# Seven pair products in two more expert half layers of an attention, expert and feed-forward kernel

## Chip, core and metric

The kernel runs on one core of a Trainium2 chip. The metric is the device time of one execution in microseconds (us); the median of three runs of the kernel before is 1067.14 us (1067.11 to 1068.03). All arithmetic is float32; a matrix product is made of three float32r products (high times high, high times low, low times high), so every operand is split into a high part (a float32r copy) and a low part (the rest).

## The reference

```python
x = attention(q, k, v, s)                  # 1152 tokens, 512 wide
P = gate(x @ w_gate)                       # exp, then 8 alternating normalisations, 1152 x 8
for e in range(8):                         # w1[e]: 512 x 1024, w2[e]: 1024 x 512
    out += P[:, e:e+1] * (np.maximum(x @ w1[e], 0) @ w2[e])
h = out @ w_in                             # 512 x 2048, given in float64
return softplus(h) @ w_out                 # 2048 x 512, given in float64
```

## The kernel before

After the attention the work is a row of 20 **half layers**, each with 512 hidden units: 0 to 15 are the experts' (two an expert), 16 to 19 the last layer's. `NX` is 16, `NH` is 20, `XE` is 2. A half layer has two parts.

**Up.** The tokens come in two groups g of 576. For each group the 512 by 512 product is made by a scheme with seven products instead of eight; the names a1 to b7 in the order strings stand for these products (two sets, a and b), each of six matmuls that move 288 columns (L450). That gives 28 products in a half layer. Vector and Scalar combine them and write the hidden values as high and low parts (`hh`, `hl`).

**Down.** In half layers 0 to 15 `downs` multiplies by w2 tile by tile: nine tiles of 128 tokens, four row blocks of w2 each, three matmuls of 512 columns for each (L526), 108 matmuls in all. One such triple is a "d" in the order strings, 36 in a half layer. After a tile's last triple Vector adds it, times the gate, to `acc` (L544). The two banks y1 and y2 alternate between tiles, so a tile can't begin before the add of the tile two before has read its bank.

In half layers 16 to 19 (`SEVEN`, `seven(x)`) the down product of the eight whole tiles also has seven products (`pairs`, L368): for each group 7 products, two row halves each, six matmuls of 256 columns, which is 14 "d" of six matmuls a group and 168 matmuls in all; only the tile that straddles the groups still goes through `downs` (12 matmuls of 512 columns). For this the hidden values are first written as whole words (`hw`, L406), then `h_steps` makes their sums (L303) and high and low parts (L296, L299), and the four sums of w2's blocks lie in `sp_t["th"]` and `sp_t["tl"]`.

**Weights.** For half layers 1 to 15 the raw weights are loaded by SP (`load`, L142) and split while the half layer before runs: `sums1` and `sums2` on GpSimd (L162 to L171) make the block sums of w1, `split` makes high parts on Scalar (L153) and low parts on Vector (L156), `prep2` does the same for w2 (L219, L221; half of the low parts on GpSimd). w2's parts have one buffer, so each row block is replaced as soon as the last tile has used it. For half layers 16 to 19 `convert` makes everything ahead: 16 jobs, each of two `narrow` (64-bit numbers made into float32 by seven Vector operations, one Scalar and one GpSimd operation), four block sums on GpSimd (L1130), and four high parts (Scalar, L1138) and low parts (Vector, L1140), stored to DRAM (`wd`, L1144). `ready1`, `prep_b` and `prep_t` later load them from there with DMAs on SP.

**Order.** The order is written by hand: `play` goes through a string; after every product and every d it calls `step`, which advances the generators of the side work by one yield: `back` (weights), `side` and `bot` (hidden values), the gate's steps in half layers up to 1, and `convert` in half layers 2 to 13 at every second step. Part A of half layer x runs products of (x, group 1) among the d of tiles 0 to 3 (30 steps), part B runs products of (x+1, group 0) among the d of tiles 4 to 8 (34 steps). Every engine works in program order, so an instruction that waits holds what is behind it.

```python
A_SEQ = "a1 b1 a2 b2 =0 d d a6 d d b6 d d a7 d d b7 =1 d a5 d b5 d a3 d b3 d a4 d b4 d d"
B_SEQ = "d d =2 a1 d d b1 d a2 d b2 d a6 d b6 d a7 d b7 d a5 d b5 d d w0 a3 d d w2 b3 d d w1 a4 d d w3 b4"
A7_SEQ = "E0 a1 ~ b1 ~ {22} a2 ~ b2 ~ {21} =0 a6 d b6 d a7 d b7 d F0 =1 a5 d b5 d a3 d b3 d a4 d b4 d"
```

`=0` to `=2` queue the splits of the next half layer's w1, `w0` to `w3` those of its w2, `E` and `F` queue `h_steps`. Where the half layer before was not a seven-product one, `~` and the braces in `A7_SEQ` are empty. At x = 14 what is left of `convert` is run and its memory closed; at the end of half layer 15 `open_blocks` takes memory for `hw`, `th` and the like.

## Time and profile before

| | us |
|---|---|
| median of three runs | 1067.14 |
| the profiled execution | 1068.36 |
| its span, first to last instruction | 1066.6 |
| TensorE busy (matmul) | 1051.5 |
| VectorE busy | 776.1 |
| ScalarE busy | 518.4 |
| GpSimd busy | 341.6 |

The profiled execution is 1.76 us longer than its span and 1.22 us above the median. Matmul records overlap, since a matmul's record lasts longer than the distance to the next; TensorE's pace is therefore read from the chain of work that ended last, where a piece's time is the distance to the next piece. TensorE's granted clock is 0.998 of full speed (2.4 GHz) on average.

### The profile page before, as it was taken

How to read it: one execution, taken by the hardware profiler on the slowest of the kernel's cores; microseconds unless marked ns; L12 is line 12 of the kernel's file. 1: busy time of each engine (PE TensorE's matmuls, PEld its weight loads, DVE VectorE, ACT ScalarE, POOL GpSimd, SP SyncE). 2: the span in 40 equal slices, each digit the busy share in tenths (PEclk: the TensorE clock that was granted, in tenths of full speed). 3: DMA queues.
4: the chain of work that ended last, by engine and by line, in shares of the span. 5: the costliest groups of instructions: out<-in, count | busy, mean ns of one | idle time of the engine just before them, and what ended most of it. 6: DMA issues, size and time to landing. Idle time of an engine off the chain costs nothing.

```text
span 1066.6 us, 18737 instructions
## 1 busy us (share of the span) xinstructions
PE 1051.5 (99%) x6876; PEld 940.2 (88%) x6876; DVE 776.1 (73%) x1713; ACT 518.4 (49%) x1232; POOL 341.6 (32%) x397
## 2 busy tenths in 40 slices
PE   6999999999999999999999999999999999999998
PEld 4777888898898888888898888888898889999998
DVE  5576565777879787898878888788555467577766
ACT  6999544344444444444444435444343247543432
POOL 8885303053543335261543434163220011000000
PEclk9999999999999999999999999999999999999999
DMA  6231101124333534334343433442220244464542
GB/s 199 75 88 57 41 29 52 41 99 128 137 126 125 178 113 164 123 115 139 148 160 101 174 121 137 129 149 75 93 80 1 63 163 151 139 209 153 172 139 89
DMA packets 75827, 124.63 MB, mean 117 GB/s; under 512 B 9184, under 2 KB 45024, under 8 KB 75736
## 3 DMA queue, kind: packets, MB, share of 16 engines
q1 hardware_dynamic: 75552, 123.23, 34.5%
q8 instruction: 54, 0.88, 0.3%
q14 instruction: 37, 0.30, 0.1%
q10 hardware_dynamic: 184, 0.20, 0.1%
HBM read 89.06 MB, written 33.82 MB: 115 GB/s over the span
## 4 chain that ended last, share of the span: by engine, by line
PE 90%; DVE 4%; POOL 2%; issue 2%; ACT 2%; DMA 1%; SPq 0%; POOLq 0%; ACTq 0%; DVEq 0%
PE ph L450 39%; PE py L526 37%; PE py L368 7%; PE sc L742 1%; PE pv L849 1%; POOL eb L805 1%; PE tr L823 1%; PE sc L746 0%; DVE w2l L221 0%; ACT eb L792 0%; DVE acc L544 0%; PE tr L817 0%; PE pv L859 0%; PE pg L1030 0%; DVE c L1105 0%
## 5 line engine op out<-in xcount | busy, mean ns | idle before, releaser
L450 PE MATMUL ph<-xh,w1h 128*128 128x288 f32 x1120 | 331.9, 296 | 0.9 <-DVE t L489 0.5
L450 PE MATMUL ph<-xh,w1l 128*128 128x288 f32 x1120 | 330.8, 295 | 0.0
L450 PE MATMUL ph<-xl,w1h 128*128 128x288 f32 x1120 | 329.3, 294 | 0.0
L526 PE MATMUL py<-w2h,hh 128*128 128x512 f32 x588 | 233.7, 397 | 0.7 <-DVE acc L544 0.7
L526 PE MATMUL py<-w2h,hl 128*128 128x512 f32 x588 | 232.5, 395 | 0.0
L526 PE MATMUL py<-w2l,hh 128*128 128x512 f32 x588 | 232.3, 395 | 0.0
L450 PEld LDWEIGHTS ph<-xh,w1h 128*128 128x128 f32 x1120 | 210.1, 188 | 19.6 <-ACT v L458 1.5
L450 PEld LDWEIGHTS ph<-xl,w1h 128*128 128x128 f32 x1120 | 210.4, 188 | 16.7
L450 PEld LDWEIGHTS ph<-xh,w1l 128*128 128x128 f32 x1120 | 210.2, 188 | 0.0
L417 ACT ACTIVATE hh<-ph 128x288 fp32r<-128x288 f32 x192 | 78.5, 410 | 165.0 <-DVE ph L500 96.1
L458 ACT ACTIVATE v<-ph 128x288 f32<-128x288 f32 x160 | 64.5, 409 | 178.2 <-PE ph L450 175.8
L526 PEld LDWEIGHTS py<-w2h,hl 128*128 128x128 f32 x588 | 110.5, 188 | 26.9 <-DVE hl L424 0.3
L544 DVE SCALAR_TENSOR_TENSOR acc<-py,gate,acc 128x512 f32<-128x512 f32 x126 | 93.7, 744 | 47.1 <-PE py L526 47.1
L526 PEld LDWEIGHTS py<-w2h,hh 128*128 128x128 f32 x588 | 110.4, 188 | 11.3 <-DVE acc L544 1.1
L526 PEld LDWEIGHTS py<-w2l,hh 128*128 128x128 f32 x588 | 110.6, 188 | 9.4
L221 POOL TENSOR_TENSOR w2l<-raw,w2h 128x512 fp32r<-128x512 f32 x32 | 44.6, 1393 | 215.2 <-ACT w2h L219 213.2
L1114 POOL TENSOR_TENSOR c<-c,ct 128x512 f32<-128x512 f32 x32 | 43.3, 1354 | 216.9 <-DVE ct L1111 198.3
L424 DVE SCALAR_TENSOR_TENSOR hl<-ph,hh 128x288 fp32r<-128x288 f32 x192 | 86.5, 452 | 28.4 <-ACT hh L417 26.7
L156 DVE TENSOR_TENSOR w1l<-raw,w1h 128x512 fp32r<-128x512 f32 (+1 forms) x128 | 89.5, 699 | 7.5 <-ACT w1h L153 7.3
L489 DVE TENSOR_TENSOR t<-ph,v 128x288 f32<-128x288 f32 x80 | 36.4, 454 | 63.6 <-ACT v L458 62.9
L153 ACT ACTIVATE w1h<-raw 128x512 fp32r<-128x512 f32 (+1 forms) x128 | 73.1, 571 | 1.6 <-POOL raw L169 1.6
L331 DVE TENSOR_TENSOR acc<-py,acc 128x256 f32<-128x256 f32 x96 | 40.6, 423 | 31.5 <-PE py L368 27.8
(237 smaller groups left out, 1704.2 us busy)
## 6 DMA issues: line engine op xcount, KB each, us to landing
raw<-in_w SPq DMA_DIRECT2D x64, 512.0 KB
wd<-ch SPq DMA_DIRECT2D x56, 256.0 KB
wd<-cl SPq DMA_DIRECT2D x56, 256.0 KB
f<-in_w_in SPq DMA_DIRECT2D x16, 512.0 KB
f<-in_w_out SPq DMA_DIRECT2D x16, 512.0 KB
w1h<-wd SPq DMA_DIRECT2D x24, 256.0 KB
w1l<-wd SPq DMA_DIRECT2D x24, 256.0 KB
th<-wd SPq DMA_DIRECT2D x16, 256.0 KB
```

Source lines behind the costliest of these rows:

```text
L153: nc.scalar.activation(out=hi[:, o], in_=t[:, src], func=AF.Copy)
L156: nc.vector.tensor_tensor(out=lo[:, o], in0=t[:, src], in1=f(hi[:, o]), op=ALU.subtract)
L221: (nc.gpsimd if i else nc.vector).tensor_tensor(out=lo, in0=t[:, r], in1=f(hi), op=ALU.subtract)
L331: nc.vector.tensor_tensor(out=a, in0=py, in1=a, op=ALU.add)
L368: nc.tensor.matmul(o, u, v, start=(start and c == 0 and n == 0), stop=(c == 1 and n == 2), skip_group_check=True)
L417: nc.scalar.activation(out=hh, in_=z, func=AF.Relu)
L424: nc.vector.scalar_tensor_tensor(out=hl, in0=z, scalar=0.0, in1=f(hh), op0=ALU.max, op1=ALU.subtract)
L450: nc.tensor.matmul(o, u, v, start=(start and c == 0 and n == 0), stop=(c == 1 and n == 2), skip_group_check=True)
L458: nc.scalar.activation(out=t, in_=self.a, func=AF.Copy)
L526: nc.tensor.matmul(py[t], u, v, start=(k == 0 and n == 0), stop=(k == NF - 1 and n == 2))
L544: nc.vector.scalar_tensor_tensor(out=a, in0=py, scalar=gate_t[0][:, t, e:e + 1], in1=a, op0=ALU.mult, op1=ALU.add)
L1114: nc.gpsimd.tensor_tensor(out=m, in0=m, in1=f(t), op=ALU.add)
```

## The change

Half layers 13 and 14 join `SEVEN`. What is stored in `wd` is now one tensor a half layer.

- **Weights of 13** are made by a new generator `prepare`, advanced at four of seven steps during half layers up to 1 (beside the gate). For each of four jobs (w1 twice, w2 twice): loads on SP, four block sums on GpSimd, four high parts on Scalar; each low part is a Scalar copy of the negated high part, onto which a DMA issued by GpSimd adds the raw weights (`accum_op`). They are stored by SP with the pool `c0`.
- **Weights of 14** are made by the same generator inside `convert`, ahead of the conversion, with the low parts on Vector.
- **`convert`** is advanced at three of four steps instead of one of two, in half layers 2 to 12, and has to be done at the end of part A of 12 (there `open_blocks` follows) instead of part A of 13. `narrow` gets two more yields, so that no two of its Vector operations come in one step, and stores are issued one block later.
- **Half layer 15** stays as it was, but follows a seven-product one: four of its w1 low parts and its four w2 low parts are made by a negated copy on Scalar and an adding DMA issued by GpSimd.
- The writing of hidden values is put off by counts that `later` gives; the loads of `th`/`tl` for 13 (`y3 y2 y4 y1`) stand in part B of 12.

```diff
-    SEVEN = (NX, NX + 1, NX + 2, NX + 3)
+    SEVEN = (NX - 3, NX - 2, *range(NX, NH))
     def load(x, which, i):
+        while seven(x):
+            x += 1
 # split
-            nc.vector.tensor_tensor(out=lo[:, o], in0=t[:, src], in1=f(hi[:, o]), op=ALU.subtract)
+            if seven(x - 1) and g < 2:
+                nc.scalar.activation(out=lo[:, o], in_=f(hi[:, o]), func=AF.Copy, scale=-1.0)
+                nc.gpsimd.dma_start(out=f(lo[:, o]), in_=t[:, src], accum_op=ALU.add)
+            else:
+                nc.vector.tensor_tensor(out=lo[:, o], in0=t[:, src], in1=f(hi[:, o]), op=ALU.subtract)
 # prep2
-        (nc.gpsimd if i else nc.vector).tensor_tensor(out=lo, in0=t[:, r], in1=f(hi), op=ALU.subtract)
+        if seven(x - 1):
+            nc.scalar.activation(out=lo, in_=f(hi), func=AF.Copy, scale=-1.0)
+            nc.gpsimd.dma_start(out=f(lo), in_=t[:, r], accum_op=ALU.add)
+        else:
+            (nc.gpsimd if i else nc.vector).tensor_tensor(out=lo, in0=t[:, r], in1=f(hi), op=ALU.subtract)
+    def later(x, g, k):
+        if seven(x):
+            return 0 if (x, g) == (NX, 0) else k
+        return 10 if k == 8 and g == 0 and seven(x - 1) else 0
+        def seven_blocks(pool, t, which, x, n, bufs, added):
...
+            for c in range(4):
...
+                nc.scalar.activation(out=h, in_=t[:, u], func=AF.Copy)
+                yield
+                if c in added:
+                    nc.scalar.activation(out=l, in_=f(h), func=AF.Copy, scale=-1.0)
+                    nc.gpsimd.dma_start(out=f(l), in_=t[:, u], accum_op=ALU.add)
+                else:
+                    nc.vector.tensor_tensor(out=l, in0=t[:, u], in1=f(h), op=ALU.subtract)
+                for _ in store:
+                    pass
+                store = put(u, h, l)
+                yield
+        def prepare(pool, xs, bufs):
+            for x in xs:
+                for which, n in ((1, 0), (1, 1), (2, 0), (2, 1)):
...
+                    for _ in range(3):
+                        yield
+                    yield from seven_blocks(pool, t, which, x, n, bufs, range(4) if bufs == 4 else ())
+                    for _ in range(2):
+                        yield
 # convert
-            for _ in range(4):
-                yield
+            yield from prepare(cv, [x for x in SEVEN[1:] if x < NX], 3)
 # step
+                if tick[0] % 7 in (1, 3, 5, 6):
+                    next(first, None)
-            elif x < NX - 2 and tick[0] % 2:
+            elif x < SEVEN[0] and tick[0] % 4:
                 next(conv, None)
 # the half layers
-            if x == NX - 2:
-                for _ in conv:
-                    pass
-                cv.close()
+            if x + 1 == SEVEN[0]:
+                for _ in conv:
+                    pass
+                cv.close()
+                own = open_blocks()
-                play(B_SEQ, products(x + 1, 0), d)
+                play(B_SEQ.replace("b2", "b2 y3 y2 y4 y1") if seven(x + 1) else B_SEQ, products(x + 1, 0), d)
```

## Rows read from the trace of the kernel before

**Rows 1.** The page: span, then busy time, share and instructions of each engine.
```profile
span 1066.6 us, 18737 instructions
...
PE 1051.5 (99%) x6876; PEld 940.2 (88%) x6876; DVE 776.1 (73%) x1713; ACT 518.4 (49%) x1232; POOL 341.6 (32%) x397
```

**Rows 2.** The page: the chain of work that ended last, by engine.
```profile
PE 90%; DVE 4%; POOL 2%; issue 2%; ACT 2%; DMA 1%; SPq 0%; POOLq 0%; ACTq 0%; DVEq 0%
```

**Rows 3.** Busy time by half layer, from one product a1 to the next half's.
```profile
core 0: us, PE busy (x) PEld busy (x) DVE busy (x) ACT busy (x) POOL busy (x), PEclk, DMA share, GB/s
...
148.13:196.40 48.27, 48.27 (x284) 43.16 (x282) 32.20 (x109) 19.68 (x45) 8.43 (x10) 1.00 0.13 44
...
339.35:387.91 48.56, 48.00 (x277) 42.52 (x276) 41.41 (x73) 21.70 (x50) 20.93 (x21) 1.00 0.40 136
...
435.39:483.32 47.93, 47.72 (x277) 42.59 (x276) 41.75 (x74) 21.42 (x50) 22.61 (x21) 1.00 0.39 135
483.32:530.80 47.48, 47.48 (x277) 42.55 (x276) 39.70 (x76) 22.10 (x50) 15.57 (x17) 1.00 0.41 142
...
578.28:626.11 47.83, 47.74 (x277) 42.48 (x276) 40.22 (x74) 23.06 (x51) 16.45 (x16) 1.00 0.46 155
...
721.07:768.55 47.48, 47.48 (x277) 42.56 (x276) 35.22 (x64) 19.63 (x45) 15.18 (x16) 1.00 0.27 89
768.55:816.03 47.48, 47.48 (x277) 42.55 (x276) 24.27 (x47) 18.74 (x41) 8.44 (x10) 1.00 0.13 45
...
911.32:956.13 44.81, 44.81 (x350) 44.27 (x349) 27.84 (x55) 21.92 (x54) 0.00 (x0) 1.00 0.54 177
```

**Rows 4.** Pieces of the chain that ended last: start us, us, what.
```profile
506.43 3.99 PE ph L450 x30
528.17 2.80 PE py L526 x12
...
922.67 1.40 PE py L368 x12
```

**Rows 5.** Who TensorE waited for from 196 to 890 us: total, times, longest.
```profile
PE py L526 <- DVE acc L544: 0.7, 2, 0.5
```

**Rows 6.** Twelve us from the start of part A: half layers 7 and 14.
```profile
459.13:471.13 12.00, 12.00 (x74) 10.81 (x72) 11.81 (x20) 5.06 (x13) 7.42 (x7) 1.00 0.38 133
...
792.29:804.29 12.00, 12.00 (x75) 10.91 (x74) 5.68 (x13) 5.01 (x11) 5.66 (x7) 1.00 0.26 89
```

**Rows 7.** Groups by line and shape: busy us, mean ns, idle before.
```profile
L1130 POOL TENSOR_TENSOR c<-c 128x256 f32<-128x256 f32 x64 | 52.7, 842 | 1.7
...
L500 DVE TENSOR_TENSOR ph<-ph,u 128x288 f32<-128x288 f32 x80 | 36.7, 459 | 19.0 <-PE ph L450 18.6
...
L1138 ACT ACTIVATE ch<-c 128x512 fp32r<-128x512 f32 x56 | 34.6, 625 | 0.9 <-POOL c L1130 0.8
...
L299 DVE TENSOR_TENSOR hl<-hw,hh 128x512 fp32r<-128x512 f32 x32 | 21.9, 685 | 1.7 <-ACT hh L296 1.5
...
L296 ACT ACTIVATE hh<-hw 128x512 fp32r<-128x512 f32 x32 | 20.0, 624 | 3.0 <-DVE hw L303 2.9
L406 ACT ACTIVATE hw<-ph 128x288 f32<-128x288 f32 x48 | 19.0, 409 | 26.3 <-DVE ph L500 14.1 <-PE ph L450 11.4 <-DVE ph L471 0.5
```

**Rows 8.** The chain at the start: the two longest pieces that are DMAs.
```profile
0.74 3.02 DMA xr<-in_s
13.26 2.71 DMA qk<-in_q
```

**Rows 9.** Issues by SP of one kind: duration ns least/median/most, first and last start.
```profile
L1144 SPq DMA_DIRECT2D wd<-ch x64: 319/378/1168, 250.6 to 750.8; - x64
```

**Rows 10.** The first Vector operation of `narrow`, in the same columns.
```profile
L1098 DVE TENSOR_SCALAR f<-f x32: 413/421/1523, 225.1 to 728.5; 128x512 f32<-128x512 f32 x32
```

More of the change, by code (lines that the diff above doesn't have):

```diff
@@ L318, in h_steps @@
                 elif n[0] == "h":
-                    assert n != "hs3" or g or not seven(last[0]) or (*last, "s4 done") in ready
+                    assert n != "hs3" or g and "s3h" in sp_t or not seven(last[0]) or (*last, "s4 done") in ready
                     high(n[1:])
@@ L1068, in gate_steps, with put @@
                 yield
+        def seven_blocks(pool, t, which, x, n, bufs, added):
+            for o, a, b, op in (((4, 0, 3, ALU.add), (6, 1, 0, ALU.subtract), (7, 4, 1, ALU.subtract),
+                                 (5, 2, 7, ALU.subtract)) if which == 1 else
+                                ((4, 1, 0, ALU.subtract), (6, 3, 1, ALU.subtract), (5, 3, 4, ALU.subtract),
+                                 (7, 2, 5, ALU.subtract))):
+                nc.gpsimd.tensor_tensor(out=t[:, o], in0=t[:, a], in1=t[:, b], op=op)
+                if o == 6:
+                    yield
+            yield
+            store = iter(())
+            def put(u, h, l):
+                for k, y in enumerate((h, l)):
+                    d = wd[1, x][n][:, k, u] if which == 1 else wd[2, x][:, k, u, n]
+                    nc.sync.dma_start(out=d, in_=f(y))
+                    yield
+            for c in range(4):
+                o = int(which == 1 and c == 0)
+                u = slice(2 * c + o, 2 * c + 2)
+                h, l = (pool.tile([P, 2, HW], F32R, tag="c" + k, name="c" + k, bufs=bufs)[:, o:] for k in "hl")
+                nc.scalar.activation(out=h, in_=t[:, u], func=AF.Copy)
[8 more added lines that the diff above has]
+                store = put(u, h, l)
+                yield
+            yield
+            for _ in store:
+                pass
@@ new lines, in prepare @@
+        def prepare(pool, xs, bufs):
+            for x in xs:
+                for which, n in ((1, 0), (1, 1), (2, 0), (2, 1)):
+                    t = pool.tile([P, 8, HW], F32, tag="c8", name="c8", bufs=1)
+                    src = ([(t[:, :4], w1[x, n])] if which == 1 else
+                           [(t[:, 2 * i:2 * i + 2], w2[x, i][:, n * DM:(n + 1) * DM]) for i in range(2)])
+                    for o, z in src:
+                        nc.sync.dma_start(out=o, in_=z.rearrange("p (b n) -> p b n", n=HW))
+                    for _ in range(3):
+                        yield
+                    yield from seven_blocks(pool, t, which, x, n, bufs, range(4) if bufs == 4 else ())
+                    for _ in range(2):
+                        yield
@@ L1217, in attention_moe_ffn @@
         conv = iter(())
+        c0 = ExitStack()
+        first = prepare(c0.enter_context(tc.tile_pool(name="c0", bufs=4, reuse_waits="tile")), SEVEN[:1], 4)
         back = []
@@ L1373, in attention_moe_ffn @@
             if x == XE - 1:
-                for _ in gates:
+                for _ in then(gates, first):
                     pass
+                c0.close()
                 gt.close()
```

56 lines of the change are left out of this document (21 added, 35 removed).

## The prediction

> **What bounds the kernel now.** First the busy times: TensorE is busy for 1051.5 of 1066.6 us, Vector is next with 776.1 [rows 1]. Since matmul records overlap, that alone proves nothing, so second the chain of work that ended last: 90% of it is TensorE [rows 2]. Third the length of each half layer. Half layers 8, 13 and 14 take 47.48 us each, to the hundredth, although Vector is busy for 39.70, 35.22 and 24.27 us of them [rows 3]: a length that doesn't move with the load of the others is TensorE's own. The pieces of the chain say the same: 2.80 us for 12 matmuls of 512 columns is 0.233 us each, 3.99 us for 30 of 288 is 0.133 [rows 4], and 168 x 0.133 + 108 x 0.233 = 47.5 us. The half layers that are longer, 5, 7 and 10, have together 1.08 + 0.45 + 0.35 = 1.88 us over 47.48 [rows 3]; they are where Vector is busiest, and what TensorE visibly waited for from 196 to 890 us is Vector's add to `acc`, twice, 0.7 us in all [rows 5]. So: TensorE bounds everything after the attention, and Vector is the engine that could take its place while `convert` runs.
>
> **What the change takes away.** A half layer with seven pair products has 168 matmuls of 256 columns where the other has 96 of 512; the other 12 and the 168 of the up product stay. 12 of 256 columns take 1.40 us, 0.117 each [rows 4]: 96 x 0.233 - 168 x 0.117 = 22.4 - 19.6 = 2.8 us. The stage itself gives a little less: half layer 17, which already has them, takes 44.81 us (18 the same), against 47.48 [rows 3], so 2.67 us. I take the stage, because it holds what the pair products cost in stalls. Two half layers: **-5.34 us**, all of it on the path.
>
> The Trainium skill (TensorE: Matmul & The Clock Gate, Back-to-back issue gap) gives a matmul its columns at 2.4 GHz plus about 2.5 ns. That makes 215.8 and 109.2 ns, and a gain of 96 x 215.8 - 168 x 109.2 = 2.4 us, an estimate from that page, or 4.7 for two; the rows have 233 and 117 ns at the full clock, so here the cost over the columns is not a fixed one, and the rows decide.
>
> **What it adds beside the path.** The steps are the clock of the side work: 64 steps in 47.48 us, 0.742 us each.
>
> (1) `convert`. Before, a job takes 22 yields at every second step: 32 yields a half layer, 1.45 jobs. After, narrow has 8 yields instead of 6 and a job 27; three of four steps are 48 yields a half layer, 1.78 jobs. Need: 4 x 16 for the weights of 14 and 16 x 27 = 496; there are 10 half layers and the 30 steps of part A of 12, 670 x 3/4 = 502. It just fits, so no burst is left for the moment when `convert` is emptied. Vector's price of one job: half layer 8 has 39.70 us of Vector work, 14 without conversion has 24.27 [rows 3], so 15.4 / 1.45 = 10.6 us. After: 24.3 + 1.78 x 10.6 = 43.2 of 47.48 us, 91%, where it was 84%; the busiest half layer so far, 7, has 41.75 us and lost 0.45 [rows 3]. So Vector still has room on average, and what counts are the stretches in which narrow runs. The tightest is early in part A: the first tile's add must free its bank within one d and one product, some 1.5 us after its last matmul, of which the add takes half. Twelve us from the start of part A, Vector has 5.68 us of work without conversion and 11.81 with narrow in it [rows 6]. Narrow's seven Vector operations come in 12 steps before and in 10.7 after, so 6.1 us become 6.9, and 11.8 become 12.6 in 12.0: 0.6 us of backlog more. Against that no step has two of them any more, which takes away up to one operation of lag. Narrow covers 16 of 27 yields, so it meets this place in about 6 of 10 half layers. Bounds: all present stalls gone, -1.9 us; every one of 10 half layers as bad as the worst now, 10 x 1.08 - 1.9 = +8.9. I take **+1.0**, near the low end, as a conversion load of 11.8 in 12 us costs a few tenths today. The weights of 14 add 16 Vector low parts in the first 64 yields; they come where narrow doesn't run yet.
>
> (2) The gate's stretch. 16 high parts and 16 negated copies on Scalar, 32 x 0.625 = 20 us; 16 block sums on GpSimd, 16 x 0.842 = 13.5 us [rows 7]; 16 adding DMAs. Scalar is busy for 19.7 us and GpSimd for 8.4 us of the 48.27 us of half layer 1 [rows 3], so both have room, and 64 of some 80 yields are needed. Such a half layer is 0.8 us over 47.48 now. I take +0.2 (0 to 1.5).
>
> (3) The adding DMA, 24 in all: no row shows a DMA that GpSimd issues. From below, an issue by SP takes 0.32 us [rows 9], and a DMA's whole way at the start of the program takes 2.71 and 3.02 us [rows 8]; from above I put 10 us to landing and one block sum's time or two on GpSimd. I take about 3 us, by rows 8, and no cost: in 14 the copies for 15 are queued 6 to 8 us ahead of the product that needs them, and w2's row block 2, the tightest, some 7 us. What is queued behind: `sums2` on GpSimd overwrites what the DMA reads, so it now waits for the landing; behind it wait the next high parts on Scalar, and behind those Scalar's copies of products. The cover is gone at about 8 us.
> The Trainium skill (DMA: Bandwidth & Descriptors, Anatomy of one DMA) gives this path 2.0 us plus the bytes at 436 GB/s: an estimate of 2.6 us for 256 KB, by which the sum stays. No run here shows it.
>
> (4) The entry into 13. Its first pair product comes five products after the last one of part B of 12, 5 x 0.8 = 4.0 us. Till then: Vector's add 0.46, the word on Scalar 0.41, high part 0.62, low part 0.685 [rows 7], in order with two of Scalar's copies, one more high part and one add, each about 0.4: some 3.6 us. It fits with little room; +0.2 (0 to 1.5). The weights of 13 come by DMA as those of 17 do now; the last block that is needed early, w1's load in the string (row block 1), is issued 3 us before the last product ends and used 4 us after that. Words, sums and parts of 13 and 14 are those of 17, whose stretch leaves Vector 17 us idle [rows 3]; the gate's factor in the 28 adds costs Vector nothing that shows. Vector loses the splits for 13 and 14, which is worth nothing.
>
> **The sum**, against the profiled execution of 1068.36 us: -5.34 + 1.0 + 0.2 + 0.2 = -3.9, so 1064.4; the median of the runs stands 1.22 us below it: **1063.2 us**. What is late next is still TensorE.
>
> **The rivals.**
> No new stall at all: 1067.14 - 5.34 = 1061.8, and with the present ones gone 1059.9. For it: no two Vector operations of narrow in one step. Chance 0.14.
>
> Vector takes the gain back: a backlog in 6 to 10 half layers at the worst loss of today, 1.08 us, and part A's first bank as the place; 6 x 1.08 - 1.9 = +4.6 gives 1066.4, 10 x 1.08 gives 1070.7 at the very most. What speaks for it is 91% on average, over 100% within narrow. One thing could make it so: the first operation of narrow takes 421 ns mostly, and 1523 at most [rows 10]; the 1.1 us between are about one GpSimd operation, and GpSimd's work per half layer grows by the same 22% as the jobs. The Trainium skill (SBUF — State Buffer, Who interferes with whom) has it that such Vector instructions and GpSimd's share a port that one of them holds to the end of its instruction; the trace agrees with its 1523. Chance 0.18, and the time lies mostly within 0.2% of no change.
>
> Slower: the adding DMA takes over about 8.7 us to land. In the gate's stretch one job's tile is loaded anew only after the last such DMA has read it; from that DMA's yield to the next job's first high part there are 9 yields of 1.3 us, 11.7, less 3 for the load. Above that Scalar stands with the high part at its head, and TensorE behind its copies; four jobs in a row, and half layer 15's weights twice. At 12 us: 4 x 3.3 + 2 x 4 = 21, less 5.3: 1083. It decides from about 11 us on (4 x 2.3 + 2 x 3 = 15). Rows 8 speak against it. Chance 0.08.
>
> **How the numbers follow.** Forecast 0.58, no new stall 0.14, Vector 0.18, DMA 0.08, others that are slower 0.02. What a measurement can tell here is 0.2%, 2.1 us: faster is under 1065.0, which the forecast mostly and the second case meet: 0.70; within 0.2%: Vector's case and the upper end of the forecast, 0.19; slower 0.11. Range: from 1060.9, between the two values without new stalls, to 1068.0, which takes in most of Vector's case and leaves the DMA's out.
>
> **What would show it.** Right: half layers 13 and 14 at about 44.8 us each, those from 2 to 12 at 47.5 to 48.1 with TensorE's waits on `acc` of one or two us in all, and no longer gate stretch. Wrong: half layers of 48.5 us and more with Vector full in their part A (Vector's case); gaps of TensorE behind Scalar in half layers 0, 1 and 14, with GpSimd waiting for DMAs (the DMA's case); a gap of over 1 us at the first pair product of 13 would undo (4).

## The result and the profile after

The changed kernel takes **1078.1 us** (four runs, 1077.5 to 1080.0), the one before 1067.1: 1.0104 times as long, interval 1.0092 to 1.0117. The forecast was 1063.2 us, its range 1060.9 to 1068.0. The profiled execution is the longest of the four (1080.0 us), so its parts add up to some 2 us more than the median.

The page of the changed kernel: span, busy time of each engine, and the chain that ended last.

```profile
span 1078.2 us, 19516 instructions
...
PE 1051.5 (98%) x7020; PEld 943.5 (88%) x7020; DVE 818.1 (76%) x1759; ACT 546.7 (51%) x1296; POOL 371.5 (34%) x431
...
PE 69%; DVE 14%; POOL 5%; DMA 4%; issue 4%; ACT 4%; SPq 0%; POOLq 0%; DVEq 0%; ACTq 0%
```

Against [rows 1, 2] TensorE's busy time hasn't moved, although its matmuls became shorter by some 5 us: records around a stall are longer, and count as busy (half layer 8 has 48.78 us for the products that took 47.48 before). Its share of the chain fell from 90 to 69%. That tells which engines the chain runs through, not how long TensorE stood; the table below has that. Busy time by half layer, in the columns of [rows 3]; these are half layers 1, 2, 4, 8, 13 and 14:

```profile
147.58:199.51 51.93, 50.05 (x283) 44.43 (x282) 36.37 (x109) 29.10 (x65) 23.39 (x29) 0.97 0.75 204
199.51:250.62 51.11, 48.12 (x278) 42.62 (x277) 32.30 (x68) 19.03 (x45) 20.37 (x23) 1.00 0.42 142
298.59:347.19 48.60, 47.75 (x277) 42.61 (x276) 44.27 (x79) 22.90 (x52) 22.87 (x22) 1.00 0.45 152
492.75:543.59 50.84, 48.78 (x278) 42.13 (x276) 44.28 (x78) 22.75 (x52) 21.78 (x22) 1.00 0.47 161
737.47:779.41 41.94, 41.94 (x283) 39.48 (x282) 20.13 (x38) 14.47 (x35) 0.00 (x0) 1.00 0.54 180
779.41:824.23 44.82, 44.82 (x351) 44.27 (x350) 32.89 (x65) 23.45 (x53) 5.51 (x7) 1.00 0.45 136
```

Cut finer, from the first product of each part to the first of the next, the two profiled executions differ like this (1A is part A of half layer 1; a row of half layer x above is part B of x - 1 and part A of x). Every part that isn't named differs by less than 0.1 us.

| stretch | after less before, us | forecast |
|---|---|---|
| attention, up to half layer 0 | -1.3 | 0 |
| parts A of half layers 0, 1, 2 | +0.7, +3.7, +3.1 = +7.4 | +0.2 |
| parts A of 3 to 11 | +0.5, +1.1, -1.1, +1.3, +1.4, +3.2, +1.3, +1.0, +1.3 = +10.0 | +1.0 |
| parts B of 2 to 12 | +0.2 | 0 |
| part A of 12 | 0.0 | 0 |
| 13A, 13B, 14A, 14B, 15A | -5.5, +0.1, -2.7, +3.5, 0.0 = -4.7 | -5.3 + 0.2 = -5.1 |
| sum | 11.6 | -3.9 |

The attention's 1.3 us have nothing to do with the change. In the profiled execution before, the granted clock is 0.50 (1.2 instead of 2.4 GHz) from 18.1 to 21.4 us, in that of the changed kernel it is 1.00:

```profile
18.10:21.40 3.30, 3.23 (x18) 2.24 (x16) 0.91 (x6) 2.94 (x10) 3.30 (x5) 0.50 0.91 351
18.10:21.40 3.30, 3.08 (x29) 2.17 (x28) 1.63 (x10) 3.29 (x11) 3.30 (x5) 1.00 0.98 361
```

Nine of the nineteen traces of this document have the low stretch there, and their attention is as long as before to 0.3 us; in the ten without it, it is 0.9 to 1.3 us shorter.

So the gain came, nearly in full, and 17 us went elsewhere, all but 0.2 of it in parts A. What TensorE waited for from 105 to 890 us (total, times, longest), where [rows 5] had 0.7 from 196 us on:

```profile
PE py L541 <- DVE acc L559: 6.3, 7, 2.3
PE ph L465 <- ACT v L473: 4.8, 6, 1.8
PE py L541 <- ACT hh L427: 1.1, 2, 0.6
```

Line numbers moved: L465 are the up products, L541 the down products, L559 the add to `acc`, L1093 the block sums of `seven_blocks`, L1102 its stores, L1109 its high parts, L1112 the negated copies, L1113 the adding DMA, L1115 its low parts on Vector.

**Half layer 1, part A**: the chain that ended last (start us, us, what) leads to a stall of TensorE that ends at 190.84. Behind it a line of Scalar's timeline, with its idle time and what ended it.

```profile
173.86 6.54 DMA cl<-c
...
180.42 0.36 SPq L1102
...
180.83 4.88 DMA c<-in_w
...
185.86 2.14 POOL c L1093 x3
...
188.81 0.69 POOL raw L175
...
190.06 0.43 ACT hh L427
190.49 0.31 ACT v L473
```

```profile
185.72 0.63 ACT L1109 ACTIVATE ch<-c 128x512 fp32r<-128x512 f32 x1 [5.38 <-DMA c<-in_w]
```

The last adding DMA of a job takes 6.54 us; SP's store of what it made stands for it; SP's next instruction, the load of the next job's tile, is queued 0.4 us behind that store and takes 4.88 us more. (The load has to wait for this DMA in any case: the tile has one buffer, and the DMA reads it.) Scalar stands 5.4 us for the tile with the job's first high part; GpSimd stands for it with four block sums and, behind them, with the sums of the next half layer's w1 (L175); Scalar stands for these with w1's high part, and the copies that TensorE needs are behind that. After this stall of 1.8 us TensorE runs for a while at half speed: from 192.1 to 195.5 us the granted clock (the column after the five engines) is 0.50, 1.2 instead of 2.4 GHz. Half of these 3.4 us is lost, an estimate of 1.7 us, and with the stall that makes 3.5 of the 3.7 us of 1A.

```profile
171.53:189.00 17.47, 17.47 (x107) 15.74 (x105) 12.17 (x37) 7.75 (x18) 8.45 (x12) 1.00 0.81 242
192.13:195.50 3.37, 3.37 (x13) 2.90 (x12) 3.23 (x10) 2.69 (x7) 2.03 (x3) 0.50 0.95 169
```

**Half layer 2, part A**: the first tile for 14's weights is queued on SP behind the conversion's two first loads (L1157), and takes 8.67 us; the same GpSimd queue stands for it.

```profile
224.25 0.42 SPq L1157
...
224.72 8.67 DMA c<-in_w
...
233.73 1.61 POOL c L1093 x2
235.34 1.14 POOL raw L168
```

**Half layers 3 to 11, parts A**: from 4A on no load is late (in 3A, 0.5 us longer, GpSimd still stands 5.3 us for the last tile of 14). The timeline of the dearest of them, 8A (start us, us, engine, line, idle before and what ended it):

```profile
530.89 3.79 POOL L1093 TENSOR_TENSOR c<-c 128x256 f32<-128x256 f32 x4
534.64 0.73 POOL L175 TENSOR_TENSOR raw<-raw 128x256 f32<-128x256 f32 x1
...
535.40 0.63 ACT L155 ACTIVATE w1h<-raw 128x512 fp32r<-128x512 f32 x1 [2.74 <-POOL raw L175]
535.94 0.43 ACT L427 ACTIVATE hh<-t 128x288 fp32r<-128x288 f32 x1
...
536.40 0.78 DVE L434 SCALAR_TENSOR_TENSOR hl<-t,hh 128x288 fp32r<-128x288 f32 x1 [2.32 <-ACT hh L427]
```

Four block sums of the conversion take GpSimd 3.8 us, the next half layer's sum comes behind them, Scalar stands 2.7 us for it, and Vector, busy without a break from 527 to 534, then stands 2.3 us for Scalar; TensorE stands 0.9 us for Scalar's copy, until 536.7. Six us earlier in the same part TensorE stood 0.4 us for Vector's add. So there were three suspects for this stretch: Vector full (theory 1), GpSimd's sums at the head of the queues (theory 5), and Scalar's waits for stores that free its buffers (theory 4). For the first stretch there was one, the late loads (theory 2).

### The profile page after: what moved, and what is told of

It is laid out like the page before. It is cut to its first block, busy times and chain, and to the rows that moved or that the text cites. A ratio compares the mean times of both kernels' runs of the same rounds, so it can differ in the third digit from the quotient of the medians.

```text
span 1078.2 us, 19516 instructions
## 1 busy us (share of the span) xinstructions
PE 1051.5 (98%) x7020; PEld 943.5 (88%) x7020; DVE 818.1 (76%) x1759; ACT 546.7 (51%) x1296; POOL 371.5 (34%) x431
## 3 DMA queue, kind: packets, MB, share of 16 engines
q1 hardware_dynamic: 100704, 154.70, 43.2%
## 4 chain that ended last, share of the span: by engine, by line
PE 69%; DVE 14%; POOL 5%; DMA 4%; issue 4%; ACT 4%; SPq 0%; POOLq 0%; DVEq 0%; ACTq 0%
PE ph L465 29%; PE py L541 22%; PE py L378 11%; DVE hl L434 2%; PE sc L757 2%; DMA c<-in_w 2%; DVE acc L559 2%; POOL c L1093 1%; DVE w1l L162 1%; POOL eb L820 1%; DMA wd<-ch 1%; PE pv L864 1%; PE tr L838 1%; DVE c L1174 1%; DVE ct L1171 1%
## 5 line engine op out<-in xcount | busy, mean ns | idle before, releaser
L465 PE MATMUL ph<-xh,w1h 128*128 128x288 f32 x1120 | 332.7, 297 | 5.7 <-ACT v L473 4.8
L465 PE MATMUL ph<-xh,w1l 128*128 128x288 f32 x1120 | 331.0, 296 | 0.0
L465 PE MATMUL ph<-xl,w1h 128*128 128x288 f32 x1120 | 329.7, 294 | 0.0
L465 PEld LDWEIGHTS ph<-xh,w1h 128*128 128x128 f32 x1120 | 210.6, 188 | 24.0 <-ACT v L473 7.6
L465 PEld LDWEIGHTS ph<-xl,w1h 128*128 128x128 f32 x1120 | 210.8, 188 | 14.6
L541 PE MATMUL py<-w2h,hh 128*128 128x512 f32 x524 | 209.9, 401 | 7.7 <-DVE acc L559 6.3
L465 PEld LDWEIGHTS ph<-xh,w1l 128*128 128x128 f32 x1120 | 210.5, 188 | 0.0
L541 PE MATMUL py<-w2h,hl 128*128 128x512 f32 x524 | 207.8, 397 | 0.0
L541 PE MATMUL py<-w2l,hh 128*128 128x512 f32 x524 | 207.4, 396 | 0.0
L541 PEld LDWEIGHTS py<-w2h,hl 128*128 128x128 f32 x524 | 98.6, 188 | 24.8 <-DVE hl L434 1.2
L541 PEld LDWEIGHTS py<-w2h,hh 128*128 128x128 f32 x524 | 98.5, 188 | 20.7 <-DVE acc L559 8.6
L541 PEld LDWEIGHTS py<-w2l,hh 128*128 128x128 f32 x524 | 98.7, 188 | 8.1
L1093 POOL TENSOR_TENSOR c<-c 128x256 f32<-128x256 f32 x96 | 80.3, 854 | 46.8 <-DMA c<-in_w 42.8
L559 DVE SCALAR_TENSOR_TENSOR acc<-py,gate,acc 128x512 f32<-128x512 f32 x110 | 81.5, 742 | 18.5 <-PE py L541 18.5
L1115 DVE TENSOR_TENSOR cl<-c,ch 128x512 fp32r<-128x512 f32 (+1 forms) x80 | 68.2, 860 | 21.4 <-ACT ch L1109 21.1
L162 DVE TENSOR_TENSOR w1l<-raw,w1h 128x256 fp32r<-128x256 f32 (+1 forms) x108 | 77.0, 713 | 5.4 <-ACT w1h L155 5.2
L1109 ACT ACTIVATE ch<-c 128x512 fp32r<-128x512 f32 (+1 forms) x96 | 56.8, 600 | 34.6 <-DMA wd<-ch 11.7
L504 DVE TENSOR_TENSOR t<-ph,v 128x288 f32<-128x288 f32 x80 | 36.2, 453 | 43.2 <-ACT v L473 42.6
```

What stands on the lines that cost most here:

```text
L162: nc.vector.tensor_tensor(out=lo[:, o], in0=t[:, src], in1=f(hi[:, o]), op=ALU.subtract)
L465: nc.tensor.matmul(o, u, v, start=(start and c == 0 and n == 0), stop=(c == 1 and n == 2), skip_group_check=True)
L541: nc.tensor.matmul(py[t], u, v, start=(k == 0 and n == 0), stop=(k == NF - 1 and n == 2))
L559: nc.vector.scalar_tensor_tensor(out=a, in0=py, scalar=gate_t[0][:, t, e:e + 1], in1=a, op0=ALU.mult, op1=ALU.add)
L1093: nc.gpsimd.tensor_tensor(out=t[:, o], in0=t[:, a], in1=t[:, b], op=op)
L1109: nc.scalar.activation(out=h, in_=t[:, u], func=AF.Copy)
```

## The experiments

Ratios are to the kernel before, measured again beside each of these kernels (medians of 1067.1 to 1068.2 us); where two kernels are compared, go by them. Lengths of parts are those of the profiled executions.

### The two halves of the change alone

Pace alone: `SEVEN` as before, three turns in four, 64 idle turns for the making.

```diff
-    SEVEN = (NX - 3, NX - 2, *range(NX, NH))
+    SEVEN = tuple(range(NX, NH))
...
-            yield from prepare(cv, [x for x in SEVEN[1:] if x < NX], 3)
+            for _ in range(64):
+                yield
...
-        first = prepare(..., SEVEN[:1], 4)
+        first = iter(())
...
-            elif x < SEVEN[0] and tick[0] % 4:
+            elif x < NX - 3 and tick[0] % 4:
...
```

> The change's new pace of the conversion alone: three steps in four, closed at the end of part A of half layer 12, with the two more yields in each narrowing; half layers 13 and 14 keep eight pair products, and no weights are made for them (the 64 turns that this would take are left idle). Theory 1 (the conversion at three turns in four fills Vector in the parts A, and that costs the 10 us that half layers 3 to 11 are longer): 1077 us, about 10 over the kernel before, spread over the parts A of 3 to 11. Theory 2 (what is lost comes from late tile loads in the stretch of half layers 0 to 2): 1067 us, as before. If Scalar's waits for the stores carry part of theory 1's loss, they are in this run too and show there.

Measured: 1076.3 us, ratio 1.0078 (1.0063 to 1.0093). The parts A of 3 to 11 are 8.9 us longer, 0A to 2A 0.4 shorter. The pace alone gives nearly all of the second stretch.

Making 13's weights alone, the conversion as before:

```diff
-    SEVEN = (NX - 3, NX - 2, *range(NX, NH))
+    SEVEN = tuple(range(NX, NH))
...
-        first = prepare(..., SEVEN[:1], 4)
+        first = prepare(..., (NX - 3,), 4)
...
-            elif x < SEVEN[0] and tick[0] % 4:
+            elif x < NX - 2 and tick[0] % 2:
...
```

> The weights for half layer 13 alone are made in the gate's stretch, with the adding DMAs, and stored, but not used: 13 and 14 keep eight pair products, and the conversion is as before. Theory 2 (the making in the gate's stretch costs time where tile loads come late behind stores on SyncE's queue): about 4 us over the kernel before (1071 us), in the parts A of half layers 0 and 1; the further 3 us of half layer 2 come from the second making and are not in this run. Theory 1: 1067 us.

Measured: 1071.3 us, ratio 1.0031 (1.0019 to 1.0043); 1A is 3.0 us longer, 2A as before. The parts A of 3 to 11 differ by -1.1 to +0.6 us, -0.8 in all; 13A is 0.9 longer, where what is left of the conversion is run at once. (It has one turn more a job here, and has to be done at the end of part A of 13; in the kernel before it has until the end of part B of 13.) So each of the two losses comes without the other.

### Late loads

Tiles for 13 loaded one job ahead (the raw half of the tile gets two buffers), the conversion's first loads behind the making of 14's weights.

```diff
-            fetch(0)
-            fetch(1)
             yield from prepare(cv, [x for x in SEVEN[1:] if x < NX], 3)
+            fetch(0)
+            fetch(1)
...
+                    if j + early < len(jobs):
+                        got[j + early] = fetch_(*jobs[j + early])
...
```

> The changed kernel, but in the gate's stretch the load of the next tile is issued one job ahead into a second buffer of its raw half (so it no longer stands behind stores that wait for an adding DMA), and the conversion's first two loads are issued behind the making of 14's weights. Theory 2: 1A and 2A lose most of their 6.8 us, 1072 to 1074 us. If the lateness of the loads is hidden anyway and Vector or Scalar is the bound in 1A and 2A too: within 1 us of 1078.

Measured: 1075.0 us. 1A is 1.4 us over the kernel before instead of 3.7, 2A 0.4 under it instead of 3.1 over; 0A to 2A together 1.1 instead of 7.4 (four other kernels whose code is as the change's up to there have 4.9 to 5.6, so the usual saving is some 4 us). TensorE's waits from 105 to 260 us, 5.4 us in the changed kernel, are

```profile
PE ph L465 <- ACT v L473: 1.1, 2, 0.8
PE pcs L1068 <- DVE csr L1082: 0.4, 1, 0.4
```

Theory 2 holds. In 2A the order alone was changed, so there it is the place behind the conversion's loads. In 1A the load got a second buffer and an earlier place together, and which of the two does it isn't shown; by the chain the place behind the store is worth 0.4 us. Half layers 3 to 11 still lose 9.3 us.

### What the parts A of 3 to 11 lack

Six kernels, each the changed one with one thing different; the last column is 3A to 11A against the kernel before.

| kernel | median us | ratio | 3A to 11A, us |
|---|---|---|---|
| the change | 1078.1 | 1.0104 | +10.0 |
| four buffers for the high part | 1078.3 | 1.0095 | +9.7 |
| block sums one by one | 1078.3 | 1.0100 | +9.8 |
| no subtraction on Vector | 1074.5 | 1.0064 | +6.7 |
| no block sums on GpSimd | 1072.1 | 1.0043 | +3.7 |
| neither | 1071.9 | 1.0036 | +2.5 |
| block sums on Vector | 1086.7 | 1.0177 | +18.8 |

"No subtraction" and "no block sums" leave these out of the computation; Scalar's copies stand in their place.

Four buffers:

```diff
-name="c" + k, bufs=bufs)[:, o:] for k in "hl")
+name="c" + k, bufs=bufs + (bufs == 3 and k == "h"))[:, o:] for k in "hl")
```

> The changed kernel with a fourth buffer for the high part in the conversion and in the making of 14's weights; nothing else differs. Theory 4 (the stores, issued one turn of the blocks later, come too late for three buffers, and Scalar's high part stands for them, 11.7 us in 7 waits of the list): the parts A of 3 to 11 lose 2 to 5 us, 1073 to 1076 us. Theory 1 (Vector is full): Scalar's waits go and the time stays within 1 us of 1078.

Scalar's waits for the stores (11.7 us from 250 to 740 us in the changed kernel) were gone from its list, and the time was 1078.3 us: those waits had been idle time that cost nothing. Theory 4 is out.

No subtraction:

```diff
+                elif x >= NX:
+                    nc.scalar.activation(out=l, in_=f(h), func=AF.Copy, scale=-1.0)
```

> The changed kernel without the subtraction that makes the low parts in the conversion (of half layers 16 to 19): Scalar writes a negated copy of the high part in its place, so Vector has 64 instructions of 0.86 us fewer and Scalar 64 of 0.64 us more. The subtraction is left out of the computation. After the first runs the 10 us of half layers 3 to 11 are two kinds of stalls of TensorE: 5.3 us in seven places end with Vector's accumulation, 4.4 us in seven others with a copy of Scalar that stood behind GpSimd's sums. Theory 1 (Vector has too much to do in a part A): the first kind goes, about 1073 us. Theory 5 (what counts is that Scalar stands in its order behind GpSimd's four block sums): within 1 us of 1078, or later, for Scalar's queue becomes longer.

1074.5 us (ratio 1.0064, 1.0049 to 1.0079). The size fits theory 1, the way only in part: from 250 to 740 us TensorE's waits for Vector's add hardly shrank (3.4 us in five places, 4.1 in six in the changed kernel), and those for Scalar's `v`, which theory 5 has, fell from 2.0 to 0.8. And Vector's amount can't be all: in the parts A of 3 to 11 it is busy for less time than in the kernel before (184.9 against 191.5 us), and 6.7 us are lost all the same. (Scalar, with the copies, has 108.3 us there instead of 89.2; what of the 6.7 us is its isn't shown.) The sums over these nine parts, before and without the subtraction (length, then the engines in the order of [rows 3]):

```profile
sum 215.54, PE 214.69 PEld 191.43 DVE 191.49 ACT 89.16 POOL 119.20; mean PE 23.85 PEld 21.27 DVE 21.28 ACT 9.91 POOL 13.24
sum 222.22, PE 216.89 PEld 190.78 DVE 184.94 ACT 108.31 POOL 120.80; mean PE 24.10 PEld 21.20 DVE 20.55 ACT 12.04 POOL 13.42
```

No block sums:

```diff
+                if x < NX:
+                    nc.gpsimd.tensor_tensor(out=t[:, o], in0=t[:, a], in1=t[:, b], op=op)
+                v = u if x < NX or c < 2 else slice(2 * c - 4, 2 * c - 2)
```

> The changed kernel without GpSimd's block sums in the conversion (4 instructions of 0.95 us a job, 16 jobs): the blocks that they make are copied from the raw halves instead, so the sums are left out of the computation and all else is issued as before. Theory 5: Scalar no longer stands behind them, the second kind of stall (4.4 us) goes, 1073 to 1074 us. Theory 1: Vector's work is the same, so its 5.3 us remain, and if it is the bound everywhere the time stays within 1 us of 1078. If GpSimd's sums also slow Vector's instructions down (1.41 us for one of 0.41 us beside them), part of the first kind goes too, down to 1069 us.

1072.1 us (ratio 1.0043, 1.0028 to 1.0058): more than theory 5's share, less than everything. Part A of half layer 8 in the changed kernel, and in this one:

```profile
516.68:543.59 26.91, 24.86 (x141) 20.94 (x139) 24.38 (x44) 11.35 (x26) 14.93 (x15) 1.00 0.42 147
```

```profile
511.85:536.42 24.57, 24.09 (x140) 21.25 (x139) 24.01 (x43) 11.88 (x27) 12.16 (x11) 1.00 0.48 161
```

Vector has as much to do as before (24.4 and 24.0 us), GpSimd four sums fewer, and 2.3 of the 3.2 us are gone. So it isn't Vector's amount alone. Over the whole kernel the sums also make Vector slower: with the same 1759 instructions it is busy for 801.6 us without them and for 818.1 with them.

```profile
PE 1047.7 (98%) x7020; PEld 942.8 (88%) x7020; DVE 801.6 (75%) x1759; ACT 548.5 (51%) x1296; POOL 317.1 (30%) x367
```

How much of what the sums cost comes by this, and how much by their place ahead of other work in GpSimd's queue, isn't separated.

Is it the burst of four sums?

```diff
-            for c in range(4):
+            for c in (0, 1, 3, 2) if which == 1 else range(4):
...
                 yield
+                if sums:
+                    sum_(*sums.pop(0))
```

> The changed kernel with GpSimd's four block sums of a job issued one by one, two ahead of the copies of the raw halves and two between them, in as many turns as before; nothing is left out and nothing else differs. Theory 5 (it is the burst of four sums, 3.8 us in one piece, behind which GpSimd's sums for the next half layer and so Scalar stand): the parts A of 3 to 11 come near the 3.7 us of the kernel without block sums, 4 to 6 us, and the time is 1072 to 1075 us. If GpSimd's whole amount of work, or its slowing of Vector, is what counted there: within 1.5 us of 1078.

1078.3 us: no, or not on the whole. 6A, 8A and 11A gained 3.7 us together, and 7A lost 2.8 more, with a stall of 2.2 us on Vector's add. Spread out, the sums stand in other places.

Both left out (the two edits together):

> The changed kernel with neither GpSimd's block sums nor Vector's subtraction in the conversion: both are left out of the computation. Each alone took 6.4 and 3.5 us of the 10.2 us in the parts A of 3 to 11. Theory A with the work of Vector and GpSimd counted together: 9 to 10 us go, about 0 to 1 us is left, 1068 to 1069.5 us. If something that neither run touched (the narrowing's seven instructions with their turns, the stores) has a share of its own: 3 to 4 us are left, about 1072 us.

1071.9 us: 2.5 us remain, so the two aren't all of it, though in 8A they are; its row is

```profile
512.51:536.25 23.74, 23.74 (x140) 21.28 (x139) 21.30 (x40) 12.87 (x30) 11.65 (x11) 1.00 0.48 167
```

with 23.74 us as in the kernel before.

The sums on Vector:

```diff
-                nc.gpsimd.tensor_tensor(out=t[:, o], in0=t[:, a], in1=t[:, b], op=op)
+                (nc.gpsimd if x < NX else nc.vector).tensor_tensor(out=t[:, o], in0=t[:, a], in1=t[:, b], op=op)
```

> The changed kernel with the conversion's block sums on Vector in place of GpSimd; nothing is left out. If GpSimd is what the parts A lack (its queue, or Vector's instructions that run slower beside its own: in the parts A of 3 to 11 Vector's 359 instructions take 38 us more than their fastest tenths): the time comes near the kernel without sums, 1072 to 1075 us. If Vector is (92% busy there, and these are 64 more instructions of some 0.4 us): 1080 us or more.

1086.7 us. Vector has no room for them: TensorE's waits for the add from 250 to 740 us rose from 4.1 to

```profile
PE py L541 <- DVE acc L559: 9.6, 7, 4.2
```

and around the one of 4.2 us, in 8A, the granted clock was 0.57 over 8 us:

```profile
535.00:543.00 8.00, 6.10 (x21) 5.44 (x22) 4.93 (x10) 1.71 (x5) 1.64 (x3) 0.57 0.23 85
```

### Adding DMAs in the conversion

```diff
-                yield from seven_blocks(cv, t, which, x, n, 3, ())
+                yield from seven_blocks(cv, t, which, x, n, 3, range(4))
```

> The changed kernel with the conversion's low parts made as in the gate's stretch: Scalar's negated copy and an adding DMA in place of Vector's subtraction. Nothing is left out. Theory 1: as the kernel without the subtraction, about 1073 us. Rival: an adding DMA holds GpSimd for 0.86 us and lands 2.7 to 6.5 us later, so the stores and with three buffers Scalar's next high part come later than now; then Scalar's waits for stores grow from 11.7 us and the time is 1078 to 1083 us.

Measured: 1151.8 us, ratio 1.0789 (1.0765 to 1.0813), far past both. Scalar's waits for DMAs from 250 to 700 us:

```profile
ACT c L1168 <- DMA cl<-c: 35.4, 8, 5.5
ACT cl L1112 <- DMA wd<-cl: 24.0, 8, 6.9
...
ACT c L1168 <- DMA wd<-ch: 9.1, 2, 4.8
```

The conversion has one tile `c8`. The next job's first Scalar operation (L1168) writes into it, and must wait until the last adding DMA has read it; Vector's subtraction takes 0.9 us (mean in the changed kernel), the DMA lands after 4.2 us (median). The second row is Scalar's negated copies, which stand until a store has freed one of the three buffers of `cl`. TensorE itself waits for Vector's add, 32.9 us in 12 places from 250 to 740 us where it was 4.1 in six; the steps between weren't traced. So the mechanism that the prediction named for the slower side exists, in a place where the change doesn't use the DMA.

### The pace itself

The turns shared out by part: seven in eight in B and five in eight in A.

```diff
-            elif x < SEVEN[0] and tick[0] % 4:
+            elif x < SEVEN[0] and (tick[0] * (5 if in_a[0] else 7)) % 8 < (5 if in_a[0] else 7):
...
```

> The changed kernel with the conversion's turns shared out by the part of the half layer: seven in eight in the parts B, five in eight in the parts A, in place of three in four in both (505 turns by the first, 502 by the second, 496 are needed). Theory 1 in its sharp form (Vector is full, whatever the order): what the parts A gain the parts B lose, within 1.5 us of 1078. If it is the density in the parts A alone, where the next half layer's weights are made too: 3A to 11A lose 10 us less some 3 to 5, the parts B stay at 23.74 us, 1072 to 1075 us.

1073.8 us: 3A to 11A lose 3.2 us, the parts B 2.7, together 5.9 instead of 10.2; 2A, where 14's weights are made, 1.0 instead of 3.1. Further the same way, the parts A at the old density:

```diff
+            elif x < SEVEN[0] and (tick[0] % 2 or not in_a[0]):
...
```

> The changed kernel with the conversion's turns as dense in the parts A as before the change (every second), and every turn in the parts B. Theory A (the density of the parts A alone decides, whichever engine stands there): the parts A of 3 to 11 are as long as in the kernel before, that is 0 where they are 10.2 us longer now, and what the parts B lose (2.7 us at seven turns in eight) grows to 4 to 8 us: 1072 to 1076 us. Theory B (each of the longer narrowing's and later store's turns costs, not their density): the parts A still lose 3 us or more.

1083.7 us, against what was expected: the parts B lose 3.7 us, but the parts A 12.6, more than at any other sharing out. Part A of half layer 3 starts at 270.2 us there, and the chain at its start is Vector's, with what part B left to do (a low part of w2, L231, of 1.44 us between two adds):

```profile
271.59 0.65 DVE cl L1115
272.24 0.38 DVE ph L515
272.62 0.51 DVE acc L559
...
273.19 1.44 DVE w2l L231
274.63 0.37 DVE hl L434
275.00 0.66 DVE acc L559
```

Here work that is moved from A to B comes back at A's first tile. So neither theory A nor B as stated: the density of the parts A alone doesn't decide.

Four in seven with 14 alone, made ahead of the conversion; two in three with both, tiles loaded ahead; both with the old narrowing:

```diff
+            elif x < SEVEN[0] and tick[0] * 4 % 7 < 4:
...
+            elif x < SEVEN[0] and tick[0] % 3:
```

> Half layer 14 alone with seven products; its weights are made ahead of the conversion, nothing in the gate's stretch, with the narrowing's turns as before the change and the side work at four turns in seven (412 of 417). Between the old pace (one in two: nothing over the kernel before) and the new one (three in four: 8.9 us). If the loss grows evenly with the pace: 2.5 us in the parts A, less 1.9 us for 14: 1067.5 to 1068.5 us. If there is a knee that four in seven stays under: 0 to 1 us, 1065.5 to 1066.5 us, the first of these kernels that is faster than the one before.

> Half layers 13 and 14 with seven products, 13's tiles loaded one job ahead in the gate's stretch, and the conversion at two turns in three with the old, shorter narrowing (two Vector instructions in some turns). If the loss grows evenly with the pace: 6 us in the parts A, 1 us in 0A to 2A, less 4.7: 1069 to 1070.5 us. If the two Vector instructions in one turn are what a dense part A can't bear: 1072 us or more. If there is a knee above two thirds: 1064 to 1066 us.

1071.4 us (ratio 1.0040, 1.0028 to 1.0053) and 1081.0 us (1.0126, 1.0110 to 1.0141). The first loses 4.7 us in 3A to 13A and 1.0 in 2A for the making, the second 16.0 us in 3A to 11A. With the old narrowing a job has 22 turns, so one turn in two, four in seven and two in three are 1.45, 1.66 and 1.94 jobs a half layer; the change, three turns in four at 27 turns a job, has 1.78. In this order, 1.45, 1.66, 1.78, 1.94, the losses against the kernel before are 0, 4.7, 10.0 and 16.0 us. With the turns spread evenly they rise steadily with the jobs a half layer; that the longer narrowing, with one Vector operation a turn, helps by itself isn't shown.

### Is there a version with a gain?

Both half layers with the three remedies (the edits above together):

> Both half layers with seven products, with the three remedies together: tiles loaded one job ahead in the gate's stretch, block sums one by one, and the conversion's turns seven in eight in the parts B and five in eight in the parts A. If the causes are separate, their gains add: the gain of 4.7 us stays, 0A to 2A cost 1 us and 3A to 11A 2 to 4 us, so 1065.5 to 1067.5 us, on a level with the kernel before. If they share one cause (the same engine time is only moved about), 1070 to 1072 us.

Measured: 1072.2 us (ratio 1.0038, 1.0026 to 1.0051). 0A to 2A cost 2.5 us, 3A to 12A 6.6 with their parts B, and the gain is 4.7: the remedies don't add. One of them even costs: with 14 alone (next two kernels) the block sums one by one make 0A to 2A 1.2 us longer.

One half layer, its tiles loaded ahead in the gate's stretch, the conversion as before:

```diff
-    SEVEN = (NX - 3, NX - 2, *range(NX, NH))
+    SEVEN = (NX - 2, *range(NX, NH))
...
-            elif x < SEVEN[0] and tick[0] % 4:
+            elif x < SEVEN[0] and tick[0] % 2:
...
```

> Half layer 14 alone with seven products; its weights are made in the gate's stretch with the tiles loaded one job ahead, and the conversion keeps its old pace of every second turn, with no more yields. By the windows of the change the gain of one half layer is 5.5 us less 3.5 us, 2.0 us, or by the count of products 2.67 us; the making costs 1 us in 0A to 2A; nothing is lost in 3A to 11A. 1065.5 to 1066.5 us, faster than the kernel before by 0.1%. Rival (the second half layer's gain needs the first): the transition out of 14 costs what it gives, 1068 us.

Measured: 1068.5 us (1067.4 to 1069.5), ratio 1.0008 with an interval from 0.9998 to 1.0017: the same as before. 3A to 11A lose nothing, 0A to 2A cost 1.7 us, and 14 gives 1.9. In this profiled execution the last store also landed 1.1 us later after the last add than in the kernel before; whether that holds for all its runs isn't shown.

The same with the block sums one by one:

> As the kernel with 14 alone, with the block sums one by one in the making and in the conversion. Theory 5: the 1.9 us that the conversion costs at its old pace in the kernel before (stalls in 5A, 7A and 10A) go too, at least in part: 1064 to 1065.5 us. Otherwise as the kernel with 14 alone.

Measured: 1069.1 us (ratio 1.0015, 1.0006 to 1.0024). 5A, 7A and 10A keep their stalls to within 0.02 us: another miss for theory 5. No version here beats the kernel before.

## Why the prediction was wrong

**What bounds the kernel, and what the change takes away**: right. TensorE's busy time stayed, and 13 and 14 became shorter by 5.3 us less 0.6. The 0.6 belongs to the way out of seven products into eight, in part B of 14, that the kernel before doesn't have. With 14 alone the gain is 1.9 us, not 2.7: it is paid once, whether one half layer is changed or two. The stage [rows 3] that gave 2.67 us lies between half layers of its own kind.

**Step (1), convert, +1.0 us: the term that failed most, +10.0 us.** Its first half was right: 43.2 us of Vector work in 47.48 were forecast, 91%; half layer 4 has 44.27 in 48.60, also 91% (4 to 11 have 41.9 to 46.0 us). The price put on that was wrong, in two ways. "Vector still has room on average" compared averages, 91% against 84%, of which the 84% cost 1.9 us; the loss rises far faster than the load. By the step's own price of a job the kernels with 1.45, 1.66, 1.78 and 1.94 jobs a half layer have Vector at 84, 88, 91 and 94%, and lose 0, 4.7, 10.0 and 16.0 us on top of the 1.9. And the upper bound, ten times the worst stall of the time, 1.08 us, took for a cap what was only the worst so far: 8A alone lost 3.2 us. The value taken lay near the low end of a range whose high end, 8.9 us, happens to be what the pace alone cost. Nor is it Vector's amount only, as the step had it: GpSimd's sums in the same part, which the step didn't count, carry a share (3.7 us left without them, 6.7 without the subtractions, 2.5 without both), and without the subtractions Vector is busy for less time in the parts A than in the kernel before. Which instruction makes the last 2.5 us isn't settled, and neither is a formula for the loss: it depends on what operation of a job falls on what place of part A, as the kernel with half the turns in A shows.

**Step (2), the gate's stretch, +0.2 us (0 to 1.5): failed, 5 to 7 us.** It went by the busy times of Scalar and GpSimd, which do have room: 29.1 and 23.4 of 51.93 us. What it didn't price is the wait for a job's tile. The rival of the slow DMA had the right chain (the tile is loaded anew only after the DMA has read it, Scalar stands with the high part at its head, TensorE behind its copies) but a threshold, a landing of 8.7 us, that was too high; the landing was never over 6.5 us. It took 3 us for the load, and in 1A it was 4.9, with 0.4 for the store ahead of it. And it took 11.7 us from the DMA to the next high part; Scalar was ready for that part 6.5 us after the DMA's start (at 180.3, 173.9). So 11.8 us stood against 6.5, and Scalar stood for 5.4. The making of 14's weights was costed for Vector's low parts only; its tile's place behind the conversion's two loads, 3.1 us in 2A, wasn't seen.

**Step (3)**, the adding DMA: 3 us to landing forecast, 3.8 us measured (median; 2.7 to 6.5); in half layer 15's weights no wait of TensorE comes from it, as forecast. **Step (4)**, the entry into 13: 0.0 us instead of 0.2 (the pieces that it adds up make 3.8 us, not 3.6; 4.0 were free).

**Rivals.** What came is the second (Vector takes the gain back), worse than its worst (10.0 us where it had 8.9), together with the third (a wait for a tile whose reader is a DMA) at a landing under its threshold. They had been taken as alternatives, with 0.18 and 0.08; they fall on different half layers (the late tiles on 0 to 2, the conversion on 3 to 11), and nothing in the profile excluded both. The signs that the prediction gave for them are what the rows show: half layers over 48.5 us with Vector busy for 24.4 of 26.9 us in part A of 8, and a gap of TensorE behind Scalar in half layer 1 with GpSimd waiting for the load behind the DMA.

## What to carry to other kernels

An engine that helps the bounding one costs little up to some load and then much (here 1.9 us at 84%, some 12 at 91%), and an average of its busy share says little on where that begins, or on which operation stands in whose way: if stalls of any size are seen at 84%, price 91% by the upper bound, not by a straight line from the lower. For every step that is moved write down each queue that it enters with the two instructions ahead of it, above all the in-order queue of the engine that issues DMAs: a load queued behind a store waits for whatever the store waits for, and one queued behind two others cost 3 us in 2A. Where a tile has one buffer, price its whole way, the last reader, the load and what is computed from it, against the time until it is needed. And before a subtraction is handed to a DMA, look how many buffers its source has, for it then stays in use until the DMA has landed.

## What the hardware showed that was not expected

- An adding DMA issued by GpSimd (14 of 256 KB, two of 128) holds GpSimd for 0.83 to 1.15 us and lands after 2.7 us at the least, 3.8 in the middle and 6.5 at the most, beside the other loads and stores of that stretch; the least is one of 128 KB, of those of 256 KB it is 3.3:

```profile
L1113 POOL DMA_DIRECT2D cl<-c x16: 832/864/1151, 118.0 to 198.2; - x16
...
DMA to landing us min/median/max: 2.7/3.8/6.5
```

The Trainium skill (DMA: Bandwidth & Descriptors, Anatomy of one DMA) would give 2.0 us plus the bytes at 436 GB/s, an estimate of 2.6 us for 256 KB from that page: all fourteen of that size are above it, by 0.7 us at the least, 1.2 in the middle and 3.9 at the worst, and the worst is what set the path.

- A stall can cost more than its length, but not each does. After 1.8 us of standing in 1A the granted clock was 0.50 from 192.1 to 195.5 us; around the 4.2 us in the kernel with the sums on Vector it was 0.57 over 8 us. After TensorE had stood 2.3 us for Vector's add in 2A, until 237.7 us, it stayed at 1.00:

```profile
237.80:243.00 5.20, 5.20 (x30) 4.50 (x30) 3.92 (x5) 1.83 (x4) 4.96 (x6) 1.00 0.53 197
```

- GpSimd slows Vector down without a wait for data. The second Vector operation of `narrow` takes 428 ns in the middle and 1421 at the most:

```profile
L1169 DVE TENSOR_SCALAR ct<-f x32: 408/428/1421, 294.9 to 715.2; 128x512 uint32<-128x512 uint32 x32
```

One that took 1.41 us, at 575.49, began 0.3 us after a GpSimd addition of 1.42 us and ended 0.3 us after its end. All 15 of the first two Vector operations of `narrow` (64 in all) that took over 0.9 us are like that: each began while a GpSimd operation ran, and ended 0.28 to 0.29 us after the end of that one. The Trainium skill (SBUF — State Buffer, Who interferes with whom) has Vector and GpSimd share a port pair that such an instruction takes as a whole, and the one that comes second waits; these pairs agree.
